# Routing of a batch in four parts, last rows copied by ScalarE, and squares of the first weights three steps behind their loads

## The chip, the cores and the metric

The kernel runs on one core of a Trainium2 chip. The metric is the device time of one execution in microseconds (us), the median of three runs. PE is TensorE, DVE is VectorE, ACT is ScalarE, POOL is GpSimd, SP is SyncE; each takes its own instructions in order, and semaphores tie them together.

## What is computed

An attention feeds a mixture of experts. q, k and v are (8 batches, 8 heads, 576 tokens, 64).

```
scores of one head: softmax(q k^T / 8) where |i - j| < 4  -> local attention
mean over 4 tokens of q, k, v -> full attention on 144 tokens -> each row repeated 4 times
x = local + repeated, as 4608 rows of 512
expert of a row: argmax of (x/|x|) (emb/|emb|)^T / tau over 8 experts; gate = its softmax share
out = gate * (relu(x w1[e]) w2[e]),  w1[e] 512 x 1024, w2[e] 1024 x 512
```

## The kernel before

**Attention.** A unit is two heads of one batch: 32 units, four to a batch. `attention` runs software-pipelined iterations i from -2 to 32. The string `ORDER` fixes in which order the operations of an iteration are issued; the table `LEAD` says how many units ahead of i each works. Scores of unit i+1, its softmax (`mx`, `sub`, `expa`, `asum`, `add`, `rec`, `an`), the transposes `wT` and copies `aT` of unit i, the products `vald` and `val` with v, and the transposes of unit i-1's result into rows (`rowsT`, `lastT`, copied by `xr` and `lastrow`) share one iteration. There is no scheduler: code order is each engine's order. In this text step i is the stretch from the start of the mask matmul (L422) of unit i+1 on PE to the next one; steps -1 to 30 cover the attention.

**Loads.** All loads of the attention go through SP's one queue: q and k for two units at a time (`load`, eight DMAs), v for the means (`load_v`, two DMAs a unit), and v in overlapping windows for two units (`load_w`, eight DMAs into the tile `vw`). `val` (L526) reads these windows. In an odd step the order on SP is `load`, the weights of that step if any, `load_w`, `load_v`. Rows of x of a finished batch go to the DRAM scratch `xd` on SP, too.

**First weights.** The expert stage needs w1 and w2 of expert 0 in half precision, as a high and a low part. The generator `first_weights` does it during attention, in pieces of 512 KB, four of w1 (`which` 0) and four of w2 (`which` 1), that share the staging tile `st`: `get` loads a piece on SP; `square` sums its squares on ACT (L824); `total` sums over partitions on PE (L832) and `scales` makes a power of two of it on DVE; `split` writes the high part on ACT (L848) and the low part on DVE (L849). A piece of w2 is loaded into the place of a piece of w1 once this is split. The table `W0` says in which steps the generator goes on: a number w there acts in step w+1, in the middle (at `Y0` of `ORDER`, ahead of `aT`). So before the change the pieces of w1 are loaded in steps 2, 3, 4 and 5 and squared in steps 7 and 8, and those of w2 are loaded in steps 11, 12, 15 and 16 and squared in steps 14 (two) and 17 (two). Splits stand in steps 11, 12, 15, 16, 19, 20, 23 and 24.

**Routing.** After the four units of batch b, `place` returns pieces of routing that the next iterations issue: `store` (at `mid`) turns the logits and sends the rows to `xd`, and at `tail`, one to an iteration, `pick` (argmax as one-hot, five DVE operations) and `rank` (position within the expert: six matmuls, eight DVE operations and five on POOL). For batch 0 they come in steps 5 and 6, for batch 1 in steps 9 and 10, and so on. In steps 27 and 28 `early_slots` builds the first lists of rows for the experts, with three wide DVE operations (L645, L649) in step 27.

**Expert stage.** 41 slots of 128 rows follow, with matmuls of 512 columns. No instruction of it is touched.

Of the kernel before, what the change touches and what calls it, by code (L numbers as in the profile page):

```python
# [58 lines left out]

W0 = (1, 2, 3, 4, 6, 7, 8, 9, 10, 11, 13, 14, 15, 16, 17, 18, 19, 22, 23)  # L60


class Kern:
# [128 lines left out]
    def attention(self, ctx):  # L192
# [26 lines left out]
        def load_v(u):  # L219
            if u < n:  # L220
                pair[u] = self.load_v(*units[u])
# [26 lines left out]
        load_v(1)  # L248
        load_v(2)
        lead = {name: k for k, names in LEAD.items() for name in names.split()}  # L250
# [9 lines left out]
        for i in range(-2, n + 1):  # L260
# [42 lines left out]
            if i + 2 < n and "late" in st[i + 2]:  # L303
                nc.vector.tensor_tensor(**st[i + 2].pop("late"))
            if i == -1:
                load(2)
                load_w(1)
                next(crows)
                self.warm_up(8)
                nc.vector.memset(self.lg, 0.5)  # L310
                nc.vector.memset(self.oh, 0.0)
# [245 lines left out]
    def op_lastrow(self, s):  # L557
        self.nc.vector.tensor_copy(out=self.row_dst(s)[:, NTB - 1], in_=s["last"])

# [14 lines left out]
    def place(self, b, xr, ls, mid):  # L574
# [6 lines left out]
        def bc(x):  # L581
            return x.unsqueeze(2).broadcast_to(shp)
# [14 lines left out]

        def pick():

            l8 = lg[:, :, :E]  # L600
            mx = rt.tile([TB, NTB], F32, name="lmx")
            v.reduce_max(out=mx, in_=l8, axis=AX.X)
            v.tensor_tensor(out=l8, in0=l8, in1=bc(mx), op=ALU.is_ge)
            v.tensor_tensor(out=l8, in0=l8, in1=self.rev, op=ALU.mult)
            v.reduce_max(out=mx, in_=lg, axis=AX.X)
            v.tensor_tensor(out=oh[:, :NTB], in0=l8, in1=bc(mx), op=ALU.is_equal)

        def rank():

# [5 lines left out]
            rk = rt.tile(shp, F32, name="rk")  # L615
            pos = rt.tile([TB, NTB], F32, name="pos")
            posi = rt.tile([TB, NTB], I32, name="posi")
            v.tensor_tensor(out=rk, in0=pk[:, :NTB], in1=self.base.unsqueeze(1).broadcast_to(shp), op=ALU.add)
            v.tensor_tensor(out=self.base, in0=self.base, in1=pk[:, NTB], op=ALU.add)
            v.tensor_tensor(out=rk, in0=rk, in1=oh[:, :NTB], op=ALU.mult)  # L620
            v.reduce_sum(out=pos, in_=rk, axis=AX.X)
            v.tensor_copy(out=posi, in_=pos)
            v.tensor_scalar(out=posi, in0=posi, scalar1=SLOT - 1, scalar2=None, op0=ALU.bitwise_and)
# [3 lines left out]
            for t in range(NTB):  # L627
                nc.gpsimd.tensor_scalar(out=self.at[:, b * NTB + t], in0=self.iota, scalar1=pm[:, t:t + 1],
                                        scalar2=None, op0=ALU.is_equal)

        if b == B - 1:
            return [store, pick, rank]
        mid.append(store)
        if b == B - 2:
            return [pick, lambda: None, rank]
        return [pick, rank]

# [219 lines left out]
    def first_weights(self):  # L857
# [13 lines left out]
        def square(which, *ps):  # L871
            for p in ps:
                self.square(tiles[p], which, p)
            if p == NP - 1:
                self.pieces_sum(which)

        def split(which, p):
            self.split(tiles[p], which, p)
            if not which:
                tiles[p] = get(1, p)  # L880

# [5 lines left out]
        yield  # L887
        square(0, 2, 3)
        yield
        self.total(slice(0, 1))  # L890
        yield
        self.scales(slice(0, 1))
        self.keep_scale()
        yield
        split(0, 0)
        yield
        split(0, 1)
        yield
        square(1, 0, 1)
        yield  # L900
        split(0, 2)
        yield
        split(0, 3)
        yield
        square(1, 2, 3)
        yield
        self.total(slice(1, 2))
        yield
        self.scales(slice(1, 2))
        split(1, 0)  # L910
# [482 lines left out]
```

## Time and profile before

| | us |
|---|---|
| median of 3 runs (761.55 to 765.26) | 762.41 |
| the profiled execution | 767.89 |
| its span, first to last instruction | 766.2 |
| PE busy in the span | 710.9 |
| DVE, ACT, POOL busy | 483.1, 462.0, 445.3 |

Times of the trace count from the start of the span. A row of a view in time order has its start, its length, the engine and line, the operation, what it writes and reads, and in brackets how long the engine sat idle before it and what ended that. An "x2" joins equal instructions that follow each other. An engine name with a q behind it is its queue, here SP issuing a DMA. A row of a stretch has its bounds, its length, the busy time (x instructions) of PE, PE's weight loads, DVE, ACT and POOL, the granted clock of PE as a share of 2.4 GHz (0.50 is the lower level, 1.2 GHz), the mean busy share of the 16 DMA engines (over 1 where packets overlap) and what they moved in GB/s.

### The profile page before, as it was taken

The page shows a single profiled execution, that of the slowest core. Times are in us where ns is not written, and L with a number is a line of the kernel's source. Part 1 is how long each engine was busy: PE and PEld are TensorE (multiplying, and loading weights), DVE is VectorE, ACT ScalarE, POOL GpSimd, SP SyncE. Part 2 cuts the span into 40 slices and gives each one's busy share as a digit, 9 for nine tenths or more (in the row PEclk, how much of TensorE's full clock was granted, in tenths as well). Part 3 has the DMA queues.
Part 4 walks back from the last instruction along what each step waited for, and adds up shares of the span by engine and source line. Part 5 has one row for each costly group of instructions (what it writes and reads, how often), then busy time and mean ns, then how long its engine had stood idle before and what let it go on. Part 6 is the DMA issues. An engine that isn't in the chain of part 4 may idle for free. (4 is left out here: it accounts for less than half of the span.)

```text
span 766.2 us, 22013 instructions
## 1 busy us (share of the span) xinstructions
PE 710.9 (93%) x7463; PEld 427.0 (56%) x7463; DVE 483.1 (63%) x1448; ACT 462.0 (60%) x1031; POOL 445.3 (58%) x853
## 2 busy tenths in 40 slices
PE   8999699886898987999999999999999999999992
PEld 5888487765787875544444444444444444444441
DVE  6778479983789877768755656466663366456320
ACT  4777657764677655455657757576775357557520
POOL 4767449691759568446666464564555563665421
PEclk7999889996899999999999999999999999999997
DMA  9789999999577826596997989989799678768840
GB/s 159 158 183 190 215 191 218 217 197 214 113 190 147 191 67 217 119 200 142 240 223 159 235 208 222 233 224 230 179 224 191 138 201 190 175 169 214 161 91 19
DMA packets 283861, 138.92 MB, mean 181 GB/s; under 512 B 250930, under 2 KB 260146, under 8 KB 283712
## 3 DMA queue, kind: packets, MB, share of 16 engines
q1 hardware_dynamic: 276992, 118.15, 72.2%
q0 software_dynamic: 6560, 19.03, 7.6%
q8 instruction: 61, 1.00, 0.6%
q14 instruction: 88, 0.72, 0.3%
q10 hardware_dynamic: 160, 0.02, 0.0%
HBM read 213.05 MB, written 20.33 MB: 305 GB/s over the span
## 5 line engine op out<-in xcount | busy, mean ns | idle before, releaser
L1245 PE MATMUL bank<-w2h,hT 128*128 128x512 f16 x328 | 124.3, 379 | 1.0 <-ACTq L990 0.9
L1210 PE MATMUL bank<-w1l,xT 128*128 128x512 f16 x328 | 124.2, 379 | 0.2 <-DVEq L990 0.2
L1246 PE MATMUL bank<-w2l,hT 128*128 128x512 f16 x328 | 124.3, 379 | 0.0
L1247 PE MATMUL bank<-w2h,hT 128*128 128x512 f16 x328 | 124.3, 379 | 0.0
L1211 PE MATMUL bank<-w1h,xT 128*128 128x512 f16 x328 | 124.3, 379 | 0.0
L1209 PE MATMUL bank<-w1h,xT 128*128 128x512 f16 x328 | 124.2, 379 | 0.0
L1106 POOL DMA_INDIRECT xg<-xd,ids x41 | 45.7, 1114 | 85.7 <-issue 34.0
L1222 ACT ACTIVATE h<-bank 128x512 f16<-128x512 f32 x82 | 48.3, 589 | 58.3 <-PE bank L1211 52.3
L824 ACT ACTIVATE junk<-st 128x1024 bf16<-128x1024 f32 (+1 forms) x30 | 67.5, 2251 | 19.6 <-DMA st<-in_moe_w_dram 15.6
L389 POOL TENSOR_TENSOR pool_kq<-kq 128x288 f32<-128x288 f32 x62 | 45.9, 741 | 54.6 <-ACT kq L380 54.6
L1258 POOL DMA_INDIRECT out_dram<-o,ids x41 | 46.1, 1125 | 49.2 <-ACTq L990 18.9
L380 ACT ACTIVATE kq<-bank 128x288 f32<-128x288 f32 x128 | 48.7, 474 | 32.8 <-PE bank L373 31.8
L1254 ACT ACTIVATE o<-bank,gt 128x512 f32<-128x512 f32 x41 | 27.8, 677 | 62.0 <-issue 19.3
L81 POOL TENSOR_SCALAR nw_t<-nw_y,nw_a 128x1 f32<-128x1 f32 x123 | 53.1, 432 | 12.4
L495 ACT ACTIVATE aT<-bank 70x384 f32<-70x384 f32 x96 | 43.6, 485 | 26.0 <-PE bank L488 22.5
L1226 DVE SCALAR_TENSOR_TENSOR h<-bank,h 128x512 f16<-128x512 f32 x82 | 56.3, 687 | 2.6 <-ACTq L999 2.2
L413 POOL TENSOR_TENSOR ld_v<-ld_v 72x256 f32<-72x256 f32 x64 | 50.0, 797 | 13.3 <-DMA ld_v<-in_v_dram 13.0
L849 DVE SCALAR_TENSOR_TENSOR w2l<-st,wscl,w2h 128x1024 f16<-128x1024 f32 x32 | 39.9, 1290 | 27.5 <-ACT w2h L848 23.4
L488 PE MATMUL bank<-ident,an 128*70 128x128 f32 x288 | 46.0, 289 | 9.7 <-DVE an L477 9.7
L1209 PEld LDWEIGHTS <-xT 128*128 128x128 f16 x328 | 35.2, 107 | 33.9
L1246 PEld LDWEIGHTS <-hT 128*128 128x128 f16 x328 | 32.1, 98 | 39.4 <-issue 1.2
L1245 PEld LDWEIGHTS <-hT 128*128 128x128 f16 x328 | 32.1, 98 | 39.0 <-DMA hT<-h 0.6
(221 smaller groups left out, 1558.9 us busy)
## 6 DMA issues: line engine op xcount, KB each, us to landing
st<-in_moe_w_dram SPq DMA_DIRECT2D x148, 1024.0 KB
ld_k<-in_k_dram SPq DMA_DIRECT2D x64, 144.0 KB
ld_q<-in_q_dram SPq DMA_DIRECT2D x64, 144.0 KB
ld_v<-in_v_dram SPq DMA_DIRECT2D x64, 144.0 KB
xd<-xr SPq DMA_DIRECT2D x8, 1040.0 KB
st<-in_moe_w_dram SPq DMA_DIRECT2D x16, 512.0 KB
vw<-in_v_dram SPq DMA_DIRECT2D x64, 122.5 KB
vw<-in_v_dram SPq DMA_DIRECT2D x32, 64.0 KB
```

The costliest lines, as they stand in the source:

```text
L81: g.tensor_scalar(out=t, in0=y, scalar1=y, scalar2=a, op0=ALU.mult, op1=ALU.mult)
L380: self.nc.scalar.activation(out=dst, in_=s["qk", r, w].rearrange("p (m i) -> p i m", m=3), func=AF.Copy, scale=(KSC, QSC)[w])
L413: self.nc.gpsimd.tensor_tensor(out=vr[:, :, 0:2 * D], in0=vr[:, :, 0:2 * D], in1=vr[:, :, 2 * D:], op=ALU.add)
L824: self.nc.scalar.activation(out=junk, in_=src, func=AF.Square, accum_out=acc)
L1209: nc.tensor.matmul(out=ps, lhsT=xT[:, 0, k], rhs=self.w1h[:, k, ns], start=(k == 0), stop=False)
L1210: nc.tensor.matmul(out=ps, lhsT=xT[:, 0, k], rhs=self.w1l[:, k, ns], start=False, stop=False)
L1211: nc.tensor.matmul(out=ps, lhsT=xT[:, 1, k], rhs=self.w1h[:, k, ns], start=False, stop=(k == self.KC - 1))
L1222: self.nc.scalar.activation(out=h2[:, 0], in_=ps, func=AF.Relu)
L1226: self.nc.vector.scalar_tensor_tensor(out=h2[:, 1], in0=ps, scalar=0.0, in1=h2[:, 0], op0=ALU.max, op1=ALU.subtract)
L1245: nc.tensor.matmul(out=ps, lhsT=hh, rhs=self.w2h[:, j, :], start=(j == 0), stop=False)
L1246: nc.tensor.matmul(out=ps, lhsT=hh, rhs=self.w2l[:, j, :], start=False, stop=False)
L1247: nc.tensor.matmul(out=ps, lhsT=hl, rhs=self.w2h[:, j, :], start=False, stop=(j == self.FC - 1))
```

## The change

It has three parts. (1) `pick` is cut into `most` and `first`, `rank` into `count` and `divide`, and for batches 0 to 4 the four parts come in four successive steps; batch 5 keeps two parts, batches 6 and 7 theirs. (2) `lastrow`, the copy of the last 64 tokens' rows out of PSUM, goes from DVE to ACT. (3) `W0` and the generator are reordered: w1's squares stand in steps 8 (two), 10 and 11, its scale in step 12, its splits in steps 13, 15, 16 and 17; w2's pieces are loaded in steps 14, 16, 17 and 18, squared in steps 19 (two), 20 and 21, scaled in step 22 and split in steps 23, 24, 27 and 28. One load of v moves behind the first iteration's code.

```diff
-W0 = (1, 2, 3, 4, 6, 7, 8, 9, 10, 11, 13, 14, 15, 16, 17, 18, 19, 22, 23)
+W0 = (1, 2, 3, 4, 7, 9, 10, 11, 12, 13, 14, 15, 16, 17, 18, 19, 20, 21, 22, 23, 26, 27)
...
         load_v(1)
-        load_v(2)
...
+            if i == -2:
+                load_v(2)
...
     def op_lastrow(self, s):
-        self.nc.vector.tensor_copy(out=self.row_dst(s)[:, NTB - 1], in_=s["last"])
+        self.nc.scalar.activation(out=self.row_dst(s)[:, NTB - 1], in_=s["last"], func=AF.Copy)
...
-        def pick():
+        def most():
...
             v.tensor_tensor(out=l8, in0=l8, in1=bc(mx), op=ALU.is_ge)
+
+        def first():
...
-        def rank():
+        def count():
...
             v.reduce_sum(out=pos, in_=rk, axis=AX.X)
+
+        def divide():
...
-        return [pick, rank]
+        return [pick, rank] if b == BEARLY - 1 else [most, first, count, divide]
...
         def split(which, p):
             self.split(tiles[p], which, p)
-            if not which:
-                tiles[p] = get(1, p)
+
+        def scale(which):
+            self.total(slice(which, which + 1))
+            self.scales(slice(which, which + 1))
...
-        square(0, 2, 3)
-        yield
-        self.total(slice(0, 1))
-        yield
-        self.scales(slice(0, 1))
+        square(0, 2)
+        yield
+        square(0, 3)
+        yield
+        scale(0)
         self.keep_scale()
         yield
         split(0, 0)
         yield
+        tiles[0] = get(1, 0)
+        yield
         split(0, 1)
         yield
+        split(0, 2)
+        tiles[1] = get(1, 1)
+        yield
+        split(0, 3)
+        tiles[2] = get(1, 2)
+        yield
+        tiles[3] = get(1, 3)
+        yield
         square(1, 0, 1)
...
```

On ACT, from the first pair of squares of w1 to the next square; `st` is the staging tile, `wss` the sums. Before, steps 7 and 8:

```order
L824 ACTIVATE junk,wss_72<-st_818 128x1024 x2
L495 ACTIVATE aT<-bank 70x384 x2
L506 ACTIVATE adT<-bank 72x3x2x48 x2
L445 ACTIVATE a<-a 128x342
L460 ACTIVATE ad,sums_107<-bank,md 96x144 x3
L495 ACTIVATE aT<-bank 70x384
L519 ACTIVATE od<-bank 128x144
L555 ACTIVATE xr<-bank 128x4x128
L380 ACTIVATE kq_103<-bank 128x96x3 x4
L824 ACTIVATE junk,wss_72<-st_818 128x1024 x2
```

And now, from the third piece's square in step 10 to the fourth's in step 11:

```order
L841 ACTIVATE junk,wss_72<-st_818 128x1024
L496 ACTIVATE aT<-bank 70x384 x2
L507 ACTIVATE adT<-bank 72x3x2x48 x2
L446 ACTIVATE a<-a 128x342
L461 ACTIVATE ad,sums_113<-bank,md 96x144 x3
L496 ACTIVATE aT<-bank 70x384
L559 ACTIVATE xr<-bank 128x128
L520 ACTIVATE od<-bank 128x144
L556 ACTIVATE xr<-bank 128x4x128
L381 ACTIVATE kq_109<-bank 128x96x3 x4
L841 ACTIVATE junk,wss_72<-st_818 128x1024
```

The two squares of step 8 now stand one by one in steps 10 and 11, and the copy of the last rows (L559) has come in ahead of `od`.

On DVE, from `md` of step 13 to the sum of the logits `ls`; `lmx` and `lg` belong to the routing of batch 2. Before:

```order
L455 TENSOR_REDUCE md<-bank 96x3
L602 TENSOR_REDUCE lmx<-lg 128x5
L603 TENSOR_TENSOR lg<-lg,lmx 128x5x8
L604 TENSOR_TENSOR lg<-lg,rev 128x5x8
L605 TENSOR_REDUCE lmx<-lg 128x5
L606 TENSOR_TENSOR oh<-lg,lmx 128x40
L464 TENSOR_REDUCE sums_107<-a 128x9
L558 COPY xr<-bank 128x128
L572 COPY ls<-bank 128x192
```

And now:

```order
L456 TENSOR_REDUCE md<-bank 96x3
L866 SCALAR_TENSOR_TENSOR w1l<-st_818,wscl,w1h 128x2x512
L603 TENSOR_REDUCE lmx<-lg 128x5
L604 TENSOR_TENSOR lg<-lg,lmx 128x5x8
L465 TENSOR_REDUCE sums_107<-a 128x9
L573 COPY ls<-bank 128x192
```

Three operations of the choice and the row copy have left this step, and a split (L866) has come in.

On DVE, from `md` to the first list operation of step 27 (`ege`, `eq`: the early lists). Before:

```order
L455 TENSOR_REDUCE md<-bank 96x3
L679 MEMSET elim 128x1 x3
L682 TENSOR_SCALAR ege<-elim,base 128x3
L683 TENSOR_REDUCE efull<-ege 128x1
L684 TENSOR_SCALAR ege<-ege 128x3
L464 TENSOR_REDUCE sums_107<-a 128x9
L558 COPY xr<-bank 128x128
L569 TENSOR_TENSOR ls<-ls,bank 128x192
L468 TENSOR_SCALAR sums_107<-sums_107 128x12
L472 RECIPROCAL sums_107<-sums_107 128x12
L645 TENSOR_TENSOR eq_5485<-sfirst,pb 128x90
```

And now:

```order
L456 TENSOR_REDUCE md<-bank 96x3
L696 MEMSET elim 128x1 x3
L699 TENSOR_SCALAR ege<-elim,base 128x3
L700 TENSOR_REDUCE efull<-ege 128x1
L701 TENSOR_SCALAR ege<-ege 128x3
L866 SCALAR_TENSOR_TENSOR w2l<-st_818,wscl,w2h 128x1024
L465 TENSOR_REDUCE sums_107<-a 128x9
L570 TENSOR_TENSOR ls<-ls,bank 128x192
L469 TENSOR_SCALAR sums_107<-sums_107 128x12
L473 RECIPROCAL sums_107<-sums_107 128x12
L662 TENSOR_TENSOR eq_5485<-sfirst,pb 128x90
```

A split of w2 (L866) stands there that was in step 23 before.

## Rows read from the trace of the kernel before

**Rows 1.** Stretches of the span, with the columns named above.

```profile
81.77:98.78 17.01, 10.29 (x165) 8.67 (x164) 7.95 (x18) 8.14 (x24) 5.15 (x9) 0.73 0.92 218
98.78:108.65 9.87, 9.87 (x170) 7.91 (x167) 5.92 (x19) 5.36 (x18) 5.01 (x9) 0.78 1.03 176
108.65:165.75 57.10, 53.79 (x1158) 43.97 (x1156) 52.47 (x122) 45.09 (x135) 47.46 (x68) 1.00 0.99 212
116.22:123.62 7.40, 7.40 (x165) 6.21 (x164) 6.85 (x14) 6.46 (x20) 7.10 (x10) 1.00 0.94 206
131.48:141.03 9.55, 8.41 (x167) 6.46 (x166) 8.88 (x20) 5.25 (x19) 7.66 (x12) 1.00 0.97 207
165.75:215.04 49.29, 37.44 (x664) 31.01 (x663) 29.09 (x77) 26.96 (x79) 25.59 (x39) 0.79 0.77 166
215.04:245.98 30.94, 30.41 (x663) 25.22 (x661) 28.27 (x69) 23.78 (x74) 24.91 (x36) 1.00 0.80 176
245.98:265.87 19.89, 17.43 (x336) 14.28 (x335) 16.65 (x46) 11.79 (x38) 11.46 (x19) 0.91 0.90 192
265.87:285.82 19.95, 17.50 (x358) 14.85 (x357) 15.68 (x41) 11.34 (x37) 12.70 (x21) 0.91 0.29 75
```

**Rows 2.** Step 8 in order of time: ACT, then PE.

```profile
89.85 1.06 ACT L824 ACTIVATE junk<-st 128x1024 bf16<-128x1024 f32 x1 [6.11 <-DMA st<-in_moe_w_dram]
...
92.48 1.23 PE L513 MATMUL bank<-adT,vd 72*64 72x144 f32 x8 [6.72 <-ACT adT L506]
...
94.69 2.19 PE L526 MATMUL bank<-aT,vw 70*64 70x64 f32 x36
```

**Rows 3.** SP's queue in order of time, around the fourth piece's load.

```profile
80.89 1.40 SPq L868 DMA_DIRECT2D st<-in_moe_w_dram  x1
...
89.59 1.15 SPq L357 DMA_DIRECT2D vw<-in_v_dram  x2
```

**Rows 4.** ACT in steps 17 and 19, in order of time.

```profile
177.41 1.06 ACT L824 ACTIVATE junk<-st 128x1024 bf16<-128x1024 f32 x1 [7.74 <-DMA st<-in_moe_w_dram]
...
198.54 1.15 ACT L848 ACTIVATE w2h<-st,wscl 128x1024 f16<-128x1024 f32 x1 [2.61 <-DVE wscl L842]
```

**Rows 5.** DVE in steps 23 and 24, in order of time.

```profile
233.76 1.27 DVE L849 SCALAR_TENSOR_TENSOR w2l<-st,wscl,w2h 128x1024 f16<-128x1024 f32 x1
...
235.37 0.28 DVE L558 COPY xr<-bank 128x128 f32<-128x128 f32 x1
236.07 0.35 DVE L569 TENSOR_TENSOR ls<-ls,bank 128x192 f32<-128x192 f32 x1 [0.43 <-ACT od L519]
...
242.28 1.27 DVE L849 SCALAR_TENSOR_TENSOR w2l<-st,wscl,w2h 128x1024 f16<-128x1024 f32 x1
```

**Rows 6.** In order of time: DVE's choice in step 13; PE in steps 25 and 28.

```profile
137.33 0.18 DVE L602 TENSOR_REDUCE lmx<-lg 128x5 f32<-128x40 f32 x1
...
139.05 0.54 DVE L606 TENSOR_TENSOR oh<-lg,lmx 128x40 bf16<-128x40 f32 x1
...
248.94 0.96 PE L488 MATMUL bank<-ident,an 128*70 128x128 f32 x6 [1.86 <-DVE an L477]
...
276.82 1.07 PE L488 MATMUL bank<-ident,an 128*70 128x128 f32 x6 [2.45 <-DVE an L477]
```

**Rows 7.** One stretch as in rows 1; then DMA issues: names, engine, count, KB each.

```profile
92.00:131.00 39.00, 38.27 (x717) 31.70 (x718) 30.64 (x79) 27.53 (x87) 26.93 (x40) 0.86 1.05 205
...
ld_k<-in_k_dram SPq DMA_DIRECT2D x64, 144.0 KB
...
xd<-xr SPq DMA_DIRECT2D x8, 1040.0 KB
st<-in_moe_w_dram SPq DMA_DIRECT2D x16, 512.0 KB
vw<-in_v_dram SPq DMA_DIRECT2D x64, 122.5 KB
vw<-in_v_dram SPq DMA_DIRECT2D x32, 64.0 KB
...
xd<-xr SPq DMA_DIRECT2D x8, 130.0 KB
```

More of the change, by code (lines that the diff above doesn't have):

```diff
@@ L596, in store @@
             save(nc.sync)
-        def pick():
+        def most():
             l8 = lg[:, :, :E]
-            mx = rt.tile([TB, NTB], F32, name="lmx")
+            mx = s["mx"] = rt.tile([TB, NTB], F32, name="lmx")
             v.reduce_max(out=mx, in_=l8, axis=AX.X)
             v.tensor_tensor(out=l8, in0=l8, in1=bc(mx), op=ALU.is_ge)
+        def first():
+            l8, mx = lg[:, :, :E], s["mx"]
             v.tensor_tensor(out=l8, in0=l8, in1=self.rev, op=ALU.mult)
@@ L615, in rank @@
             rk = rt.tile(shp, F32, name="rk")
-            pos = rt.tile([TB, NTB], F32, name="pos")
-            posi = rt.tile([TB, NTB], I32, name="posi")
+            pos = s["pos"] = rt.tile([TB, NTB], F32, name="pos")
             v.tensor_tensor(out=rk, in0=pk[:, :NTB], in1=self.base.unsqueeze(1).broadcast_to(shp), op=ALU.add)
@@ L621, in rank @@
             v.reduce_sum(out=pos, in_=rk, axis=AX.X)
+        def divide():
+            pos, posi = s["pos"], rt.tile([TB, NTB], I32, name="posi")
             v.tensor_copy(out=posi, in_=pos)
@@ L629, in rank, with pick @@
                                         scalar2=None, op0=ALU.is_equal)
+        def pick():
+            most()
+            first()
+        def rank():
+            count()
+            divide()
+        s = {}
         if b == B - 1:
@@ L900, in first_weights @@
         yield
-        split(0, 2)
+        square(1, 2)
         yield
-        split(0, 3)
+        square(1, 3)
         yield
-        square(1, 2, 3)
+        scale(1)
         yield
-        self.total(slice(1, 2))
-        yield
-        self.scales(slice(1, 2))
         split(1, 0)
```

## The prediction

> **What bounds the kernel now.** First I cut the span into the attention and expert stages and the attention into its 32 steps; a step is the time from one mask matmul on PE (TensorE) to the next. No instruction of the expert stage moves, so only attention steps count. The reader is to see in [rows 1] that a quiet step takes 7.40 us with PE busy for all of it, and that the excess over 7.40 is lumped: step 8 takes 17.01, step 9 then 9.87, steps 17 to 20 together 49.29 (four quiet ones would be 29.6), step 13 takes 9.55, steps 25 and 26 together 19.89, steps 27 and 28 together 19.95.
>
> Next, who ends those waits. In step 8 ACT (ScalarE) stands 6.11 us in front of the square of the fourth weight piece until its DMA lands, and PE, which needs the attention weights that ACT would have copied next, stands 6.72 us [rows 2]. In step 17 the same happens on the second weights, 7.74 us on ACT, and in step 19 ACT waits 2.61 us for VectorE's (DVE's) scale [rows 4]. PE then runs on at the lower of its two clock levels for a while: granted clock 0.73 and 0.78 in steps 8 and 9, 0.79 over steps 17 to 20, 1.00 in quiet steps [rows 1].
>
> Why is the piece late? Its load stands in step 5 of the program, but SP (SyncE) issues it at 80.89 us, at the end of step 7: SP has run some 2.5 steps behind PE. And behind it on the same queue stand eight loads of v windows (vw), of which the last two leave SP at 89.59 to 90.74 [rows 3]. That is the number I weigh most: the matmuls of step 8 that read these windows cannot start much before 91.7, whatever ACT does: the bounds are 90.74, with no time to land, and 94.69, where they started [rows 2]; I take an estimated 1 us to land. So of step 8's stall only part is ACT's; the rest is the queue's.
>
> **The queue's ledger.** From 92 to 131 us, a stretch with no weights in it, the engines moved 205 GB/s with their share at 1.05 [rows 7]: full. I take that rate. What has to land from 92 us until the matmuls on v windows of step 24, by the issue sizes in [rows 7] (1 KB is 1024 bytes; q has k's size, v too): eight sets of q and k of 8 x 144 KB, eight sets of windows of 4 x 122.5 + 2 x 64 KB and two small ones (620 KB), sixteen units of v of 2 x 144 KB, four batches of x rows of 1040 + 130 KB, four pieces of second weights of 512 KB: 25.5 thousand KB, 26.2 MB. At 205 GB/s that is 127.5 us, so not before 219.5. The step ends some 2 us later, near 222, where it ended at 245.98 [rows 1]. Nothing on any engine can make the first 25 steps more than **24 us** shorter unless the queue runs faster than in its full stretch.
>
> **The change, part by part.**
>
> *Squares.* Each square now stands three to six steps behind its load, so the two waits on ACT (6.11, 7.74) and, since the scale is now made a step ahead of its first use, the 2.61 of step 19 go. What is late next: in step 8 the v windows, at 91.7 for 94.69, which is 3.0 saved. Of the slow-clock time behind it (step 9 took 9.87, and 4.1 us passed from 94.69 to the next step) I take 2.0 back, since PE still idles near 4 us; the bounds are 0 and 4.3 (9.87 - 7.40, and some 1.8 of the 4.1). Steps 8 and 9 give **5.0**. Steps 17 to 20: a quiet step is 7.40, and I put 7.5. Two squares together are 2.4 us on ACT ahead of the copies that PE needs; I charge 0.6 in step 19. Step 17 now also holds a split (next paragraph), 9.0. Sum 9.0 + 7.5 + 8.1 + 7.5 = 32.1 against 49.29: **17.2** saved.
>
> *Splits and routing on DVE.* Half of the choice of experts takes at most 1.1 us (five instructions from 137.33 to 139.59, [rows 6]); I take 0.75 for a quarter of the routing. Between the splits of steps 23 and 24 DVE needs 8.52 us (233.76 to 242.28, [rows 5]), so a split already makes DVE the bound by 1.1. The new table puts splits into steps 13, 15, 16, 17, 23 and 24, each with a quarter of the routing, where most splits stood in steps without. So the routing is not moved off busy steps; the sum of DVE's work is the same.
>
> *Last rows on ACT.* The copy goes from DVE (0.28) to ACT, which has a like one (the copy of the downsampled output, which in these rows ends DVE's wait). DVE does the row copy at 235.37, ends it at 235.65, and then idles 0.43 for that ACT copy, which reads the same bank after it [rows 5]. In a step that DVE bounds both go: **0.7** a step. In a quiet step it costs and gives nothing: ACT's wait is filled by the new copy, and PE hides both. If ACT were the later one, it would cost 0.3 a step.
>
> So a step with split and quarter comes to 8.52 - 0.7 + 0.75, near 8.5; steps 13 and 17, which have the store too, to 9.55 - 0.7 + 1.27 - 1.1 = 9.0 from step 13 of before. Steps 10 to 16: 9.0 + 2 x 8.5 + 4 x 7.5 = 56.0 against 57.10, **1.1** saved. Steps 21 to 24: 7.6 + 7.5 + 8.5 + 8.5 = 32.1 against 30.94, **1.2 lost**. Steps 25 and 26 keep a whole choice and a whole rank; the wait of 1.86 before them [rows 6] falls by 0.7, and I take **1.0** saved (0 to 2.5, the larger if the clock then stays up). Steps 27 and 28 receive two splits that they did not have, ahead of the early lists that already make PE wait 2.45 [rows 6]; 1.27 + 0.3 for its slowing of others - 0.7 gives **0.9 lost** (0 to 2.5).
>
> *The moved load of v* leaves SP's order as it was; I cost it at nothing. The second weights' loads stand later in SP's order, and the ledger has them.
>
> Sum: 5.0 + 17.2 + 1.1 - 1.2 + 1.0 - 0.9 = 22.2. Up to step 24 it is 22.1, two short of the ledger's 24. With two limits that close, each will now and then wait for the other; I take 1.2 off: **21 us**. The profiled execution took 767.9 us, 5.5 above the median of 762.4; from it I come to 747, and for the median I take the same 21 off: **741 us**. If part of those 5.5 us is a longer wait for DMA, the gain in ordinary runs is smaller; the range allows for that.
>
> **A rule against the ledger.** The rows show a full queue at 205 GB/s [rows 7]. The Trainium skill (DMA: Bandwidth & Descriptors, Anatomy of one DMA) gives about 2.0 us a transfer plus bytes at 436 GB/s, fitted on another issue path. By that, as an estimate, the 26 MB would need 60 us and not 127, and the first rival below would be the forecast. The rows speak against it by a factor of two.
>
> **The rivals.** (a) *The queue has room*: PE, not DMA, sets steps 8 to 24. Then v windows are there in time and steps 8 and 9 take 15.5 in place of 26.88, 11.4 saved for my 5.0, and the 1.2 is not lost: 28.6, **734**. For it: PE hardly ever waits for q, k or v in the quiet steps [rows 1]. Against it: share 1.05, and the lag of SP. (b) *The stall moves*: with SP still 2.5 steps late, three steps are thin. Three second-weight pieces and a batch of x rows, 2.7 MB, 13 us of queue, stand in steps 16 to 18. If the squares of steps 20 and 21 each wait 3 us and the clock falls behind each by another 2.5, 11 goes: **752**. (c) *DVE takes over*: seven steps (13, 15, 16, 17, 23, 24, 27) hold a split beside other extra work. If in each PE waits as in step 28, 2.45 us and then the low clock, a step loses 5.2 (19.95 - 2 x 7.40), 36 in all where I charged 9. With 21 gained otherwise, the kernel ends 6 slower, **768**. It decides from a wait near 1.9 us: after 1.86 the clock fell, to 0.91 over steps 25 and 26 [rows 1, 6]; in steps 10 to 16, all at 1.00, it did not [rows 1]. (d) *Nothing lasting*: stalls and DVE eat the gain to within 0.5%.
>
> **How the numbers follow.** Forecast 0.56, (a) 0.13, (b) 0.19, (c) 0.05, (d) 0.07. Half a percent, 3.8 us, is about what a measurement of this kernel can tell from no change. Faster by more: forecast, (a) and (b), 0.88; within it 0.07; slower by more 0.05. The range runs from 732, two under (a), to 755, three over (b); (c) and (d) stay out.
>
> **What would show it.** Right: no ACT wait for a weight piece above 1 us; step 8 still at 13 to 14 us with PE idle until about 91.7 for v windows; steps 17 to 20 near 32; step 25 starting between 222 and 228 us; DVE's wait after the row copy gone. Wrong: step 8 under 10 us (the queue had room); PE waiting for v windows, q or k in steps 19 to 24, or ACT for the third and fourth piece (b); granted clock under 1.00 in steps 13 to 17 or 23 (c); any difference in the expert stage.

## The result and the profile after

The changed kernel takes **741.3 us** (median of 4 runs, 740.38 to 744.11) against 763.45 of the kernel before in the same comparison: a ratio of 0.9716, 95% interval 0.9678 to 0.9755. The profiled execution takes 744.11, its span is 742.4; in before these were 767.89 and 766.2. The forecast time was 741. The sum behind it was right in its total and wrong in two of its terms, which cancel: that the total came out so close is luck in part.

The stretches of the changed kernel, cut at the same mask matmuls and with the columns of [rows 1]: steps 8; 9; 10 to 16; 17 to 20; 21 to 24; 25 and 26; 27 and 28; then, as in [rows 7], a long stretch.

```profile
81.52:94.46 12.94, 10.69 (x166) 8.78 (x163) 6.21 (x16) 7.95 (x24) 7.28 (x13) 0.76 0.93 215
94.46:103.24 8.78, 8.78 (x167) 7.09 (x165) 4.94 (x14) 5.42 (x19) 5.83 (x10) 0.87 1.26 162
103.24:157.02 53.78, 53.44 (x1160) 44.32 (x1158) 46.75 (x121) 44.38 (x141) 42.27 (x64) 1.00 0.90 193
157.02:198.75 41.73, 36.36 (x662) 30.43 (x661) 30.16 (x69) 27.64 (x85) 27.82 (x44) 0.84 0.92 208
198.75:230.86 32.11, 32.11 (x664) 26.55 (x662) 24.93 (x68) 25.27 (x80) 20.54 (x32) 0.94 1.01 199
230.86:247.83 16.97, 15.71 (x337) 12.89 (x335) 16.12 (x41) 11.40 (x39) 13.12 (x22) 1.00 0.88 169
247.83:265.69 17.86, 16.09 (x359) 13.45 (x357) 16.95 (x43) 13.27 (x41) 15.99 (x22) 1.00 0.88 204
92.00:231.00 139.00, 133.22 (x2661) 110.71 (x2661) 108.09 (x272) 103.92 (x324) 98.41 (x150) 0.92 0.96 197
```

Against [rows 1] the difference of the spans, 23.8 us, comes apart like this:

| stretch | before | after | saved | forecast |
|---|---|---|---|---|
| up to step 8 | 81.77 | 81.52 | 0.3 | 0 |
| steps 8, 9 | 26.88 | 21.72 | 5.2 | 5.0 |
| steps 10 to 16 | 57.10 | 53.78 | 3.3 | 1.1 |
| steps 17 to 20 | 49.29 | 41.73 | **7.6** | **17.2** |
| steps 21 to 24 | 30.94 | 32.11 | -1.2 | -1.2 |
| steps 25 to 28 | 39.84 | 34.83 | **5.0** | **0.1** |
| behind step 28 | 480.4 | 476.7 | 3.7 | 0 |

Steps 17 to 20 first. In order of time: PE in step 17, then SP's load of the third piece of w2, ACT's square of it in step 20, and PE behind that.

```profile
165.42 1.19 PE L374 MATMUL bank<-ident,ld_q 96*128 96x96 f32 x6 [1.54 <-DMA ld_q<-in_q_dram]
...
182.30 1.32 SPq L885 DMA_DIRECT2D st<-in_moe_w_dram  x1
...
189.81 1.06 ACT L841 ACTIVATE junk<-st 128x1024 bf16<-128x1024 f32 x1 [3.39 <-DMA st<-in_moe_w_dram]
...
192.45 1.23 PE L514 MATMUL bank<-adT,vd 72*64 72x144 f32 x8 [2.56 <-ACT adT L507]
```

Both of the old stalls of ACT (6.11 us in [rows 2], 7.74 in [rows 4]) are gone, but smaller ones have come: PE waits 1.54 us for q of unit 20, and ACT 3.39 us for a piece whose load stands in step 17 of the program and leaves SP at 182.30, in step 19, two steps late. PE waits 2.56 us behind ACT, and the clock is 0.84 over these four steps. This is what the prediction described as rival (b), for the square of step 20; the wait that (b) put into step 21 did not come.

Step 8 went as forecast: PE stands before the v windows, and no longer before ACT. The first row is PE in step 7; the last shows that the windows came one by one.

```profile
79.61 1.15 PE L374 MATMUL bank<-ident,ld_q 96*128 96x96 f32 x6 [0.97 <-DMA ld_q<-in_q_dram]
...
89.16 0.66 PE L527 MATMUL bank<-aT,vw 70*64 70x64 f32 x6 [1.76 <-DMA vw<-in_v_dram]
90.22 2.33 PE L527 MATMUL bank<-aT,vw 70*64 70x64 f32 x30 [0.40 <-DMA vw<-in_v_dram]
```

On DVE, two split steps (15 and 16), from one split to the next, with the columns of [rows 5]:

```profile
145.52 1.27 DVE L866 SCALAR_TENSOR_TENSOR w1l<-st,wscl,w1h 128x1024 f16<-128x1024 f32 x1
...
147.35 0.50 DVE L465 TENSOR_REDUCE sums<-a 128x9 f32<-128x342 f32 x1
147.77 0.34 DVE L570 TENSOR_TENSOR ls<-ls,bank 128x192 f32<-128x192 f32 x1
148.03 0.49 DVE L469 TENSOR_SCALAR sums<-sums 128x12 f32<-128x12 f32 x1
...
150.96 0.72 DVE L483 TENSOR_TENSOR ad<-ad,sums 96x432 f32<-96x432 f32 x1
...
153.09 1.27 DVE L866 SCALAR_TENSOR_TENSOR w1l<-st,wscl,w1h 128x1024 f16<-128x1024 f32 x1
```

In [rows 5] a row copy of 0.28 and a wait of 0.43 stood between `sums` and `ls`; both are gone. The cycle from split to split is 7.57 us with a quarter of the routing in it, where it was 8.52 without one.

### The profile page after: what moved, and what is told of

Same layout as the page of the kernel before. It is cut to its first block, busy times and chain, and to the rows that moved or that the text cites. A ratio compares the mean times of both kernels' runs of the same rounds, so it can differ in the third digit from the quotient of the medians.

```text
span 742.4 us, 22020 instructions
## 1 busy us (share of the span) xinstructions
PE 704.1 (95%) x7463; PEld 423.1 (57%) x7463; DVE 471.3 (63%) x1416; ACT 465.0 (63%) x1063; POOL 444.9 (60%) x853
## 5 line engine op out<-in xcount | busy, mean ns | idle before, releaser
L390 POOL TENSOR_TENSOR pool_kq<-kq 128x288 f32<-128x288 f32 x62 | 42.8, 691 | 39.8 <-ACT kq L381 39.8
L866 DVE SCALAR_TENSOR_TENSOR w2l<-st,wscl,w2h 128x1024 f16<-128x1024 f32 x32 | 39.6, 1280 | 27.1 <-ACT w2h L865 27.1
L1272 PEld LDWEIGHTS <-hT 128*128 128x128 f16 x328 | 32.1, 98 | 39.4 <-issue 1.2
L1235 PEld LDWEIGHTS <-xT 128*128 128x128 f16 x328 | 35.2, 107 | 33.9
L1271 PEld LDWEIGHTS <-hT 128*128 128x128 f16 x328 | 32.1, 98 | 39.0 <-DMA hT<-h 0.6
L1237 PEld LDWEIGHTS <-xT 128*128 128x128 f16 x328 | 32.0, 98 | 39.1 <-issue 0.4
```

The source lines that it names most:

```text
L1235: nc.tensor.matmul(out=ps, lhsT=xT[:, 0, k], rhs=self.w1h[:, k, ns], start=(k == 0), stop=False)
L1237: nc.tensor.matmul(out=ps, lhsT=xT[:, 1, k], rhs=self.w1h[:, k, ns], start=False, stop=(k == self.KC - 1))
L1271: nc.tensor.matmul(out=ps, lhsT=hh, rhs=self.w2h[:, j, :], start=(j == 0), stop=False)
L1272: nc.tensor.matmul(out=ps, lhsT=hh, rhs=self.w2l[:, j, :], start=False, stop=False)
```

## Experiments: what each part is worth

Three theories stood against each other. **A**: the weights' new places take the stalls, the row copy gives the rest. **B**: the new places give all. **C**: the routing gives what steps 10 to 16 won. Each part was then built alone, and the row copy undone. All of these kernels keep the moved load of v, which was never built by itself: what it is worth, if anything, is in each of them. Each was compared with the kernel before once more, whose median then differed by some us (765.84 here), so kernels are compared by their ratios and not by their medians.

**Weights alone** (against the changed kernel):

```diff
-        self.nc.scalar.activation(out=self.row_dst(s)[:, NTB - 1], in_=s["last"], func=AF.Copy)
+        self.nc.vector.tensor_copy(out=self.row_dst(s)[:, NTB - 1], in_=s["last"])
...
-        return [pick, rank] if b == BEARLY - 1 else [most, first, count, divide]
+        return [pick, rank]
```

> The changed kernel with last rows copied by VectorE and routing in two parts again: only the new places of the first weights are left (and the moved load of v). In the profile of the changed kernel steps 8 and 9 gave 5.2 us, steps 10 to 16 3.3, steps 17 to 20 7.6 (I had forecast 17.2), steps 25 to 30 6.6 (I had forecast 0.1). Theory A (weights for the stalls, row copy for the rest): this kernel keeps the gains of steps 8, 9 and 17 to 20, some 13 us, and loses 2 to 4 in steps 27 and 28, which hold a split and the row copy on VectorE: 751 to 754 us, with the clock falling in steps 25 and 28 as before. Theory B (the new table alone makes the room, the row copy costs nothing either way): 741 to 744 us, steps 25 to 30 as short as in the changed kernel.

Measured: ratio 0.9784 (0.9740 to 0.9828), median 751.82. Its steps 17 to 20 and 21 to 24:

```profile
159.52:193.65 34.13, 31.20 (x663) 25.20 (x661) 28.52 (x71) 26.18 (x80) 25.97 (x39) 1.00 0.96 214
193.65:230.51 36.86, 33.15 (x664) 27.34 (x663) 28.08 (x75) 25.21 (x77) 24.85 (x36) 0.91 0.87 193
...
197.64 1.10 PE L431 MATMUL bank<-kq 64*32 64x38 f32 x53 [3.36 <-issue]
```

The median lies in A's range, but the ratio makes it 747 on the scale on which the changed kernel takes 741.3 (0.9784 of 763.45), between A and B. Nor did the clock fall in both places as A said: steps 25 and 26 take 17.27 us at 1.00, steps 27 and 28 take 21.19 at 0.92. Steps 17 to 20 come close to the forecast 32.1, but a stall stands in step 21 instead, in front of which the profile shows no wait for a load or another engine (the last row; "issue"), and step 25 starts at 230.51: in the changed kernel it was 230.86. What this pause of PE is stays open.

**Routing alone** (the kernel before with `most`, `first`, `count` and `divide` for batches 0 to 4, and the moved load of v):

```diff
-        return [pick, rank]
+        return [pick, rank] if b == BEARLY - 1 else [most, first, count, divide]
```

> The kernel before with only the routing of batches 0 to 4 in four parts over four steps (and the moved load of v). Both stalls of ScalarE for weight pieces remain. Theory A: the sum of VectorE's work is the same, steps that held a whole choice get shorter by up to 2 (step 13), and what is won before a stall is lost in it: 761 to 764 us, no difference that can be told. Theory C (the four parts are what shortens steps 10 to 16): those seven steps take 54 us in place of 57.1, and the kernel 758 to 761.

Measured: ratio 0.9950 (0.9923 to 0.9977), median 762.07. Steps 10 to 16, 17 to 20, and 25 and 26:

```profile
106.23:161.21 54.98, 53.27 (x1158) 44.09 (x1156) 49.94 (x125) 44.82 (x135) 41.40 (x64) 1.00 0.97 212
161.21:211.64 50.43, 38.67 (x665) 32.09 (x663) 28.27 (x76) 27.28 (x80) 23.86 (x39) 0.76 0.73 163
...
244.11:261.48 17.37, 15.92 (x337) 12.81 (x335) 15.86 (x43) 11.31 (x38) 13.37 (x23) 1.00 0.79 203
```

Half of a percent in all, which is C's time (759.6 of 763.45), but the trace reads like A: steps 10 to 16 are 2.1 us shorter, and by step 25 that is lost again, in steps 17 to 24. From the start of step 8 this execution needs 165.03 us to step 25 (244.11 - 79.08), and before needed 164.21 (245.98 - 81.77). So it is not shown which steps the half percent comes from, nor whether it is the routing's or the moved load's. The last row is the surprise. No instruction of steps 25 and 26 differs from the kernel before, and yet they take 17.37 us at full clock where the profiled execution of before took 19.89 at 0.91.

**Row copy alone** (the kernel before with `lastrow` on ACT, the first pair of lines of the first diff above the other way round, and the moved load of v):

> The kernel before with only the copy of the last rows moved from VectorE to ScalarE (and the moved load of v). Theory A: 0.7 us in each step that VectorE bounds, and where PE's wait falls from 1.9 or 2.5 us to under 1.8 its clock stays at full speed too, so steps 25 to 30 take 50 to 52 us in place of 57.8 and steps 10 to 16 some 55; the gain ahead of the stall of step 17 is lost in that stall: 754 to 757 us in all. Theory B: 761 to 764 us. By what I predicted (0.7 a step in three or four steps, no clock): 759 to 761.

Measured: ratio 0.9955 (0.9925 to 0.9985), median 764.28. Steps 25 and 26, then 27 and 28, and PE in step 28:

```profile
246.31:263.77 17.46, 15.81 (x337) 12.84 (x335) 15.60 (x42) 11.43 (x39) 11.68 (x19) 1.00 0.97 207
263.77:283.75 19.98, 17.49 (x359) 14.79 (x357) 15.00 (x39) 11.53 (x39) 12.75 (x21) 0.91 0.33 84
...
274.75 1.47 PE L489 MATMUL bank<-ident,an 128*70 128x128 f32 x6 [2.49 <-DVE an L478]
```

A is refuted in its second half: with the moved load of v the copy is worth half a percent, and not the 6 us of steps 25 to 30. PE's wait in step 28 is 2.49 us, where it was 2.45 in [rows 6]: moving the copy did not shorten it.

**The changed kernel without the row copy's move** (the first pair of lines of the first diff above):

> The changed kernel with the last rows copied by VectorE again. Theory A: the gains of steps 25 to 30 go (6 to 7 us), some 2 of those of steps 10 to 16, and steps 23 and 24, with a split, get longer: 748 to 752 us. Theory B: 741 to 744 us. In the prediction's terms a split step without this move costs 0.7 more, seven such steps: 746.

Measured: ratio 0.9731 (0.9700 to 0.9762), median 744.95, so the move cannot be told from nothing here (0.9716, its own interval 0.9678 to 0.9755). The weights alone gave 16.5 us (2.16% of 765.84, 13.2 to 19.9), the routing 3.8 (1.8 to 5.9), the row copy 3.4 (1.1 to 5.7): 23.7 together, for 21.8 by the ratio of the whole (2.84%). So nothing speaks against the parts adding up; but the intervals are wide, and the sum counts the moved load three times.

## Experiments: what sets the pace up to step 24

The ledger of the prediction gave a bound: before the bytes have passed the queue, step 24 cannot end. Theory **Q** says more: the bytes set the pace, whatever stands where; theory **S** is that a piece is late because it stands behind others on SP, so that a better place removes its wait for good.

**Second pieces an eighth as large:**

```diff
-            nc.sync.dma_start(out=t, in_=src)
+            if which:
+                nc.sync.dma_start(out=t[:16], in_=src[:16])
+            else:
+                nc.sync.dma_start(out=t, in_=src)
```

> The changed kernel, but each load of a second-weight piece brings only 16 of its 128 partitions (the output of expert 0 is then wrong): 4 x 448 KB, 1.8 MB or 9 us at 205 GB/s, leave the queue, and no instruction moves. Theory Q (bytes on the queue set the pace up to step 24): in the changed kernel PE waited for q and k in step 17 and ScalarE 3.39 us for the third piece in step 20; both waits go, step 25 starts at 220 to 225 us (changed kernel 230.9), and the kernel takes 731 to 735 us. Theory S (a piece is late because SP issues it some two steps late, however small): the wait in step 20 stays at 2 us or more and the kernel takes 738 to 742.

Measured: ratio 0.9594 (0.9564 to 0.9623), median 733.86. Steps 17 to 20, then 21 to 24:

```profile
158.64:191.16 32.52, 31.16 (x664) 25.40 (x661) 26.79 (x66) 26.65 (x85) 26.23 (x41) 1.00 0.98 193
191.16:222.00 30.84, 30.56 (x665) 25.52 (x663) 27.73 (x72) 25.37 (x81) 23.25 (x35) 1.00 0.93 200
```

Q's numbers: with 1.8 MB less and every instruction in its place, steps 17 to 20 take the 32 us of the forecast, at full clock.

**Second pieces from ACT's queue:**

```diff
-            nc.sync.dma_start(out=t, in_=src)
+            (nc.scalar if which else nc.sync).dma_start(out=t, in_=src)
```

> The changed kernel with the four second-weight pieces issued from ScalarE's queue in place of SP's. Theory S: they are issued in their own step and no longer stand behind 15 to 20 other loads; the third lands before step 20, q and k of step 17 are in time, and the kernel takes 734 to 738 us. Theory Q: the same bytes pass the same DMA engines, so what the pieces win the loads of q, k and v lose; waits of PE for q, k or v windows take the place of ScalarE's, step 25 starts at 228 to 232, and the kernel takes 739 to 744.

Measured: ratio 0.9718 (0.9685 to 0.9751), median 743.76, the changed kernel's time again. The first piece leaves at once, and PE waits for v windows in its place (step 16):

```profile
134.85 0.40 ACTq L885 DMA_DIRECT2D st<-in_moe_w_dram  x1
...
161.51 0.48 PE L527 MATMUL bank<-aT,vw 70*64 70x64 f32 x4 [2.19 <-DMA vw<-in_v_dram]
...
203.27:233.64 30.37, 30.37 (x665) 25.44 (x663) 26.89 (x72) 25.43 (x81) 21.88 (x34) 1.00 0.98 205
```

The last row, steps 21 to 24, shows that they went at PE's own pace; step 25 nevertheless starts no earlier, at 233.64. S is refuted for this kernel: the pieces no longer stand behind others, and the waits have gone over to v windows.

**Half of the loads of q and k left out:**

```diff
-            if j < n // 2:
+            if 4 <= j < n // 2 and j % 2:
+                half[j] = half[j - 1]
+            elif j < n // 2:
                 half[j] = self.load(j // 2, j % 2)
```

> The changed kernel without the loads of q and k for units 10 and 11, 14 and 15, and so on to 30 and 31; these units read those of the two units before (their results are then wrong). 1.18 MB or 5.8 us of queue leave every fourth step pair from step 6 on, four of them ahead of step 24. Theory Q: the last v windows of step 8 leave SP some 5 us earlier, so the wait for them goes and steps 7 to 9 take 23 to 25 us (changed kernel 31.3); steps 17 to 21 take 38 to 42 (changed kernel 51.2); step 25 starts at 211 to 216, and the kernel takes 721 to 727. If PE, VectorE and ScalarE set the pace instead: 738 or more.

Measured: ratio 0.9513 (0.9476 to 0.9550), median 728.12. Steps 8 and 9, then 17 to 20:

```profile
79.08:95.36 16.28, 15.67 (x330) 12.71 (x329) 13.50 (x34) 13.41 (x43) 14.02 (x22) 1.00 0.84 175
...
151.76:186.37 34.61, 32.65 (x664) 26.56 (x661) 26.86 (x66) 26.66 (x84) 25.41 (x41) 0.95 0.78 175
```

With the bytes gone steps 8 and 9 take 16.28 us, near the 15.5 that the prediction gave to a queue with room. The stall of step 8 is the queue's. Step 25 starts at 216.72, just behind Q's 211 to 216. By the trace five sets of q and k, 5.9 MB, are missing ahead of the windows of step 24, one of them ahead of step 8 (the expectation counted four in all). At 205 GB/s that is some 29 us of queue, and step 25 is only 14.1 us earlier: with so few bytes the queue no longer sets the pace.

**Other places for the weights.** The runs that follow keep all bytes. First the second weights later: loads in steps 18 to 21, squares to step 24.

```diff
-W0 = (1, 2, 3, 4, 7, 9, 10, 11, 12, 13, 14, 15, 16, 17, 18, 19, 20, 21, 22, 23, 26, 27)
+W0 = (1, 2, 3, 4, 7, 9, 10, 11, 12, 14, 15, 16, 17, 18, 19, 20, 21, 22, 23, 24, 26, 27, 28)
...
         square(1, 3)
-        yield
         scale(1)
...
```

> The changed kernel with the second weights later: loads in steps 18 to 21 (were 14, 16, 17, 18), squares in steps 22 (two), 23 and 24, the scale in step 24, splits in steps 25, 27, 28 and 29 (were 23, 24, 27, 28). Nothing else moves. Theory Q: three pieces fewer are due by step 17, so q and k of step 17 are in time, and the third piece no longer stops ScalarE in step 20; what is left of the bytes falls into steps 25 to 28, where the loads of q and k had 7 to 12 us to spare; steps 17 to 24 take 64 to 69 us (changed kernel 73.8), two splits in steps 25 and 29 cost up to 1 us each: 734 to 739 us. Theory S: only the place of the waits changes, 740 to 744.

Measured: ratio 0.9744 (0.9723 to 0.9765), median 744.81, outside what Q said and near S. The profiled execution is an unusual one of this kernel: 752.97 us, 8.2 above the median. Steps 17 to 20, steps 21 to 24, then ACT and PE in step 24:

```profile
157.52:189.01 31.49, 30.64 (x663) 25.34 (x661) 26.86 (x66) 23.67 (x78) 25.79 (x41) 1.00 0.86 205
189.01:231.10 42.09, 35.59 (x665) 29.14 (x663) 28.74 (x73) 27.59 (x86) 25.70 (x41) 0.87 1.04 211
...
220.22 1.06 ACT L841 ACTIVATE junk<-st 128x1024 bf16<-128x1024 f32 x1 [5.53 <-DMA st<-in_moe_w_dram]
...
221.61 0.58 PE L849 MATMUL bank<-wsq,onesf 128*128 128x1 f32 x2 [4.90 <-DVE wsq L844]
```

In it steps 17 to 20 have no stall left, and step 24 has all of it. Here my own arrangement did harm as well: the sum over partitions (L849) stood on PE right behind the late square, so that PE waited 4.90 us.

**Second weights one step earlier than that** (loads in steps 17 to 20, scale in a step of its own):

> The changed kernel with the second weights loaded in steps 17 to 20 (were 14, 16, 17, 18; the kernel with loads in steps 18 to 21 had steps 17 to 20 at 31.5 us but then waited 5.5 us on ScalarE for the fourth piece in step 24, and PE with it, as the sum over partitions on PE stood right behind that square). Squares in steps 21 (two), 22 and 23, the scale a step later in step 24, splits in steps 25, 27, 28 and 29. Theory Q (bytes on the queue, and then lead enough): SP runs two steps late, so three steps between a load and its square are just enough; steps 17 to 24 take 62 to 66 us (changed kernel 73.8), steps 25 to 30 some 53 (51.2): 733 to 737 us. Theory S (waits only move): some load of q, k or v is late in steps 18 to 23 in place of a weight piece: 740 to 744.

Measured: ratio 0.9686 (0.9639 to 0.9734), median 741.6. Q is missed here, too: the third piece was late again, in step 22 (ACT waits 3.09 us for it), and steps 17 to 24 take 72.29 us for Q's 62 to 66.

**First weights spread too:**

```diff
-W0 = (1, 2, 3, 4, 7, 9, 10, 11, 12, 14, 15, 16, 17, 18, 19, 20, 21, 22, 23, 24, 26, 27, 28)
+W0 = (1, 3, 5, 7, 9, 10, 11, 12, 13, 14, 15, 16, 17, 18, 19, 20, 21, 22, 23, 24, 26, 27, 28)
```

> The kernel of the run before this (second weights loaded in steps 17 to 20), and the first weights' loads spread too: in steps 2, 4, 6 and 8 (were 2, 3, 4, 5), squares in steps 10 (two), 11 and 12, scale in step 13, splits in steps 14 to 17. Theory Q: about one and a half pieces fewer, some 3 to 4 us of queue, stand ahead of the v windows of step 8, so steps 7 to 9 take 25 to 28 us (changed kernel 31.3); the bytes come back in steps 9 to 13, where q and k had 6 to 11 us to spare but the v windows 1.4 to 3.4, so 0 to 3 us of it is given back: 1 to 5 us faster than the run before this. Theory S: the wait moves from step 8 to a later one at the same cost, no difference.

Measured: ratio 0.9725 (0.9673 to 0.9777), median 746.67. In the profile steps 8 and 9 take 15.23 us and step 25 starts at 224.89, 3.6 earlier than in the run before; but the kernel as a whole was not measured faster, so Q's gain of 1 to 5 us is not shown.

**And the second squares a step later still:**

> The kernel with both weights' loads spread (first weights loaded in steps 2, 4, 6, 8, second in steps 17 to 20), and the second weights' squares a step later again: steps 22 (two), 23 and 24, scale in step 25, splits two at a time in steps 27 and 29. In the kernel with squares from step 21 on ScalarE waited 2.95 us for the third piece in step 22 and PE ran steps 22 and 23 in 22.2 us in place of 15. Theory Q: that wait goes, but the bytes due by step 24 are the same, so step 25, which there started at 224.9 us, starts between 220 and 224, the rest of the 7 us being taken by later waits or none; two splits in one step cost VectorE 1 to 2 us in steps 27 and 29: 737 to 743 us. Theory S (only positions count): all 7 us are won, step 25 starts before 219: 732 to 736.

Measured: ratio 0.9729 (0.9697 to 0.9762), median 742.52. Step 25 starts at 224.20, just above Q's 220 to 224, where all 7 us won would have meant less than 219; the waits for weight pieces are gone, and steps 21 to 24 take 36.18 us all the same. What PE waits for in step 24 are the v windows of that step:

```profile
219.20 0.34 PE L527 MATMUL bank<-aT,vw 70*64 70x64 f32 x4 [0.86 <-DMA vw<-in_v_dram]
...
221.81 0.48 PE L527 MATMUL bank<-aT,vw 70*64 70x64 f32 x4 [0.73 <-DMA vw<-in_v_dram]
```

Of all kernels with all bytes, this is the one that runs against the ledger's bound in the step for which it was worked out.

**Last, only the first weights spread**, the second as in the changed kernel (the 68 to 72 and the 105 us for steps 10 to 21 in the expectation are slips of mine; what was meant is 104.9 by S, and 111 for no gain at all):

> The changed kernel with only the first weights' loads spread: in steps 2, 4, 6 and 8 (were 2, 3, 4, 5), squares in steps 10 (two), 11 and 12, scale in step 13, splits in steps 14 to 17, the second weights' loads in steps 15 to 18 (were 14, 16, 17, 18) and from there on as in the changed kernel. With the loads spread, steps 8 and 9 took 15.2 us (changed kernel 21.7). Theory Q: the bytes due by step 24 are the same, so a good part of these 6 us comes back as waits in steps 10 to 21 (68 to 72 us in steps 10 to 21 by theory S, 105 or more by Q would be needed for no gain at all; changed kernel 104.9): step 25 starts at 225 to 230 us (changed kernel 230.9), the kernel takes 737 to 742. Theory S: step 25 starts at 224 to 225, all that steps 8 and 9 win stays: 734 to 736.

Measured: ratio 0.9665 (0.9634 to 0.9696), median 737.73. This is the lowest time of all kernels that compute everything, faster than before beyond doubt; from the changed kernel (0.9678 to 0.9755) its interval does not separate it. Steps 8 and 9, 10 to 16 and 17 to 20, and the wait that stayed:

```profile
83.24:98.47 15.23, 15.23 (x331) 12.66 (x329) 12.95 (x33) 11.46 (x39) 13.34 (x22) 1.00 1.02 196
98.47:154.45 55.98, 53.88 (x1160) 44.34 (x1158) 48.01 (x120) 46.54 (x145) 42.76 (x65) 1.00 0.85 202
154.45:194.11 39.66, 33.55 (x662) 27.54 (x661) 30.05 (x70) 27.19 (x85) 29.21 (x44) 0.93 1.03 217
...
185.37 1.06 ACT L841 ACTIVATE junk<-st 128x1024 bf16<-128x1024 f32 x1 [5.13 <-DMA st<-in_moe_w_dram]
```

Steps 8 and 9 won 6.5 us against the changed kernel; step 8 starts 1.7 later, and steps 10 to 20 take 95.64 for 95.51. Step 25, at 226.35, starts 4.5 earlier: inside Q's 225 to 230 and a little above S's 224 to 225. On the stretch that was to part the two, steps 10 to 21, S is right: it takes 105.36 us, where S meant 104.9 and Q said that a good part of 6 us would come back. In this profile what steps 8 and 9 won stayed won; in the time, 737.73, Q's range holds and S's does not.

Put side by side, in one profiled execution each: when SP issues the last two v windows of step 24 (the start of their row), and when step 25 starts.

| kernel | last windows issued (us) | step 25 starts (us) |
|---|---|---|
| changed kernel | 222.36 | 230.86 |
| weights alone | 217.57 | 230.51 |
| without the row copy's move | 219.47 | 227.66 |
| second pieces on ACT's queue | 223.99 | 233.64 |
| second weights later (steps 18 to 21) | 219.34 | 231.10 |
| second weights in steps 17 to 20 | 220.76 | 228.50 |
| both weights spread | 217.50 | 224.89 |
| the same, squares a step later | 218.02 | 224.20 |
| first weights spread only | 217.30 | 226.35 |
| second pieces an eighth as large, 1.8 MB less | 212.69 | 222.00 |
| half of q and k left out, 5.9 MB less by step 24 | 197.35 | 216.72 |

Nine kernels with all bytes and the weights out of their old order put their waits in steps 7 and 8, 16, 17, 20, 21, 22 or 24, and none starts step 25 before 224.2 in its profile; the two with fewer bytes do. The ledger's bound was 219.5 for the windows and near 222 for the step. The executions took up to 8.2 us more than their kernel's median, so a difference of a few us between two rows is not shown.

The first column hardly moves as long as the bytes are the same, 217.30 to 223.99: that much of Q holds, and it is the ledger's bound. The second column has its own spread, 224.2 to 233.64. Where a cause shows in the trace, it is the place of a load: a piece, a window or a q that is late stops PE some steps before step 24, while SP goes on issuing. So the strong form of Q, whatever stands where, does not hold, and S holds for single waits; neither is the whole.

## Why the prediction was right and where it was not

**The queue's bound held.** In the profiles no placement started step 25 before 224.2, and taking bytes away went to 222.0 and 216.7. The bound is an estimate, good to a few us: from 92 to 231 us the queue moved 197 GB/s at a share of 0.96, for the 205 that I used, and between 92 us and the last window of step 24 the nine kernels move 198 (changed kernel) to 208 GB/s (first weights spread only). But 205 was not the fastest stretch: at the 212 of steps 10 to 16 in [rows 1] the same 26.2 MB give 215.6 for the windows and near 218 for the step.

**By its own signs** the forecast failed in steps 17 to 24: ACT waited 3.39 us for a weight piece where it was to wait no more than 1, steps 17 to 20 took 41.73 for "near 32", and step 25 started at 230.86, behind "between 222 and 228". Step 8 (12.94 for 13 to 14) and DVE's wait after the row copy (gone) came out as said.

**Steps 8 and 9: right, for the reason given.** 5.2 us for 5.0, PE before v windows; the kernel without half of q and k shows whose wait it is. Four other kernels that have the same instructions up to step 9 take 20.71 to 22.72 us there, for the 21.72 of this execution. Not foreseen: PE waits 0.97 us for q in step 7.

**Steps 17 to 20: wrong, 7.6 us for 17.2.** The step that failed is "the two waits on ACT (6.11, 7.74) ... go", with 9.0, 7.5, 8.1 and 7.5 us put down for the four steps and no wait for a load in any of them. I placed the second weights' loads in the ledger as a sum over 25 steps, and met the bound by taking off 1.2 us. But three of these loads stand within steps 16 to 18, SP runs two steps late, and a distance of three steps from load to square leaves one. So the third piece and q of step 17 were late. With seven eighths of the second pieces taken away these steps took 32.52. Rival (b), with 0.19, named this mechanism and its steps; it was the true case for these steps. Up to step 24 the terms gave 22.1, and step 25 came 15.1 earlier (245.98 - 230.86): the 1.2 us for "each will now and then wait for the other" is the term that was mis-sized, and should have been 7.0.

**Steps 25 to 28, and behind: wrong the other way, 8.7 us for 0.1.** These gave back nearly all of the 9.6 us that steps 17 to 20 fell short, and most of it is no work of the change. The kernel with only the routing in four parts has before's instructions from step 25 on, and from there to its end it takes 513.8 us (757.9 - 244.11) where before took 520.2 (766.2 - 245.98) and the changed kernel 511.5 (742.4 - 230.86). So 6.4 of the 8.7 us come and go without any change behind step 24: the wait of 1.86 us and the clock of 0.91 in steps 25 and 26 [rows 1, 6] were not there in the other. One execution is one draw, here as well: the kernel with the row copy alone takes 520.0 us from step 25 on (766.3 - 246.31), and in the profiles of all fourteen kernels this part takes between 510.6 and 521.7. The step that failed is that I priced these rows as the kernel's, and thought of the 5.5 us by which that execution exceeded the median only as a longer wait for DMA.

By the ratios, which are free of that, the total is right for another reason. The two stalls were to give 22.2 us; all that the weights' new places gave, with the cost of their splits in it, is 16.5. The routing was to give nothing, and the row copy something in split steps alone; with the moved load of v in each they measure 3.8 and 3.4.

**DVE: too dear.** I put 8.5 us for a split step with a quarter of routing, and 9.0 for step 13. Between the splits of steps 15 and 16 the cycle is 7.57. Against the 8.52 of [rows 5] the quarter adds 0.64 (146.71 to 147.35), the row copy's move takes 0.71, and the rest, 0.9, is that three operations (`sums`, `an`, `ad`) were stretched in the rows that I took my price from. Two of them there, and then the first operation of the quarter in the changed kernel; the same two take 0.49 and 0.72 above:

```profile
236.34 0.86 DVE L468 TENSOR_SCALAR sums<-sums 128x12 f32<-128x12 f32 x1
...
239.78 1.09 DVE L482 TENSOR_TENSOR ad<-ad,sums 96x432 f32<-96x432 f32 x1
...
146.71 0.19 DVE L622 TENSOR_TENSOR rk<-bank,base 128x40 f32<-128x40 f32 x1
```

PE is busy for all of those 7.57 us and DVE for 7.36, so the cycle is as much PE's as DVE's, and what DVE needs at least is not shown by it. Steps 10 to 16 gained 3.3 for 1.1, and the routing with the moved load measures 0.5% (0.9923 to 0.9977) where the prediction gave it no gain of its own.

**Row copy: right in the mechanism, its worth open.** The wait for `od` is gone. Built with the moved load alone it measures 0.45% (0.15 to 0.75); undone in the changed kernel it cannot be told from nothing (0.15%), where seven split steps at 0.7 us would have been 0.64%.

**Steps 21 to 24: the number was right, the reason not.** 1.2 us lost, but to the low clock behind step 20 (0.94 over these steps, PE busy throughout), not to DVE: with the small second pieces the same instructions take 30.84 us at 1.00.

**The rivals.** (a), a queue with room, is refuted: in the changed kernel PE waits for v windows and q, and ACT for a piece, and every other placement has such waits. (c) did not come: the clock is 1.00 over steps 10 to 16, and its point, a wait near 1.9 us behind which the clock falls, is none (below). (b) was half of the truth: right in mechanism and steps, but the rest of the kernel did not stay as it was.

## What to carry to other kernels

Where a stall is a late load, add up the bytes that must land by then and divide by the rate of a stretch in which the queue was full: this estimates how much any reordering can win, and here none of nine kernels won more. Then look at each piece, for the bound alone does not say where the time comes out: with SP two steps late, three steps from load to square were too few in six of the seven kernels that had them, and four were enough in the one that had four. A stretch at low clock in one profiled execution is not yet a cost: ask whether it stands in a second one before it becomes a term of the sum.

## What the runs showed of the hardware

**The same wait, and the clock falls or does not.** PE's wait for DVE in step 28 is 1.92 us in the kernel with half of q and k and in the one with both weights spread. The first pair of rows is the one, the second the other: the wait, then steps 27 and 28 with the granted clock as the first of the last three columns.

```profile
243.16 0.82 PE L491 MATMUL bank<-ident,an 128*70 128x128 f32 x6 [1.92 <-DVE an L480]
...
232.74:250.60 17.86, 15.94 (x360) 13.30 (x357) 17.16 (x43) 13.23 (x41) 15.99 (x22) 1.00 0.31 79
```

```profile
252.76 0.99 PE L489 MATMUL bank<-ident,an 128*70 128x128 f32 x6 [1.92 <-DVE an L478]
...
242.35:261.76 19.41, 17.50 (x358) 14.80 (x357) 16.72 (x41) 13.43 (x41) 15.83 (x22) 0.91 0.83 191
```

One keeps 2.4 GHz, the other loses 1.6 us of PE time to the lower level. In the kernel with squares a step later a wait of 2.76 us there (at 253.75) left steps 27 and 28 at 1.00. The length of one wait does not tell.

**A second issuing queue gave nothing**: 0.9718 from ACT's queue, 0.9716 from SP's. The Trainium skill (DMA: Bandwidth & Descriptors, Issuing engines are not separate DMA queues) says that all of them run on the same 16 DMA engines; the two times agree.

**Beside a split on DVE an addition on POOL takes longer.** In the changed kernel POOL's addition beside the split at 145.52 takes 1.98 us, and 0.43 where no split stands. The three of its kind that run beside a split take 1.86 to 1.98, the 28 others 0.42 to 0.58:

```profile
145.10 1.98 POOL L401 TENSOR_TENSOR kdT<-pool_kq 128x144 f32<-128x144 f32 x1
...
236.92 0.43 POOL L401 TENSOR_TENSOR kdT<-pool_kq 128x144 f32<-128x144 f32 x1
```

The Trainium skill (SBUF — State Buffer, Who interferes with whom) names the case: a DVE instruction with two SBUF inputs against a GpSimd one that reads SBUF. These two rows agree. That it also is what stretched DVE's operations in [rows 5] was only argued.
